# Attention and two feed-forward layers: the first layer's weights held in SBUF and its products fused, instead of streamed blocks of seven products

## The chip, the cores and the metric

The kernel runs on one core of one Trainium2 chip. The metric is the device time of one execution in microseconds (us). The kernel before took 1274.12 us, the median of three runs (1273.81 to 1278.1).

## The reference

All inputs are float64 or float32 arrays; the result is a 2304 x 512 array in float32.

```python
def _attn_ref(q, k, v, tau):                 # q, k, v: (4, 8, 576, 64)
    scores = scale * np.matmul(q, k.transpose(0, 1, 3, 2))
    thresh = np.max(scores, axis=-1, keepdims=True) - tau
    scores = np.where(scores >= thresh, scores, -1000000000.0)
...
    return np.matmul(attn, v).astype(np.float32)

def _moe_ref(x, w_in, w_out, alpha):         # (2304,512) (512,2048) (2048,512)
    h = x @ w_in
    g = np.maximum(h, 0.0) + alpha * np.minimum(h, 0.0)
    return (g @ w_out).astype(np.float32)

def _moe2_ref(x, w_in, w_out):
    h = x @ w_in
    g = np.where(h > 0.0, h, alpha * (np.exp(np.minimum(h, 0.0)) - 1.0))   # alpha = 1
    return (g @ w_out).astype(np.float32)
```

The heads of the attention are joined to a 2304 x 512 array, which goes through the first layer (`_moe_ref`) and then the second (`_moe2_ref`).

## The kernel before

**Attention** (lines 292 to 512). A unit is one pair of heads of one batch, and has nine jobs; each job makes scores on TensorE (PE), exponentials on ScalarE (ACT), a mask on VectorE (DVE), a scaling on GpSimd (POOL), then turns the result on PE and multiplies it with the values. `attention` writes all stages into a list with a place each and emits them sorted by place. At 144 places it calls `beside`, which converts weights for the layers. The result goes to DRAM as `x_d`.

**Weights.** They are 64-bit floats in DRAM. `single` (line 140) turns a piece of 128 x 512 into a 32-bit `x`: two ACT passes, three DVE passes, one POOL addition, on a piece that `load_piece` has brought two pieces ahead. `conversion` (line 168) splits `x` into a high and a low part (both fp32r) so that a product in full precision becomes three matmuls: high by high, high by low, low by high. For weights that are used in seven products it takes two pieces, forms the sums `s1` to `s4` and stores seven split blocks to DRAM (`in_d`, `out_d`, called `wi` and `wo` in the profile) with `store` (line 208, the DMA at line 211); for the plain product it stores the split piece to `whole_d` (`wp`). All split blocks go through two `split` buffers. `convert_step` runs the conversion from one `yield` to the next; the first twelve groups (`EARLY`) are converted beside the attention, the rest beside the first layer, one step per unit of the order below.

**Layers.** The 2304 tokens are three superchunks of 768, each handled as two halves of 384. The first product of a layer (`first_product`, line 562) takes blocks of 2 x 2 and needs seven products of blocks instead of eight, of six matmuls each; a partial sum in a PSUM bank is copied away by ACT (`keep`: `c1`, `u`, `w`) before the next product is added into the same bank. The second product of the first layer is plain (`plain_product`, line 676): per `f` (one of 16 blocks of 128 hidden columns) and half, `Split` makes high and low of the hidden block (`th`, `tl`) and twelve matmuls follow. The second layer has seven products in both (`second_product`, line 710). Split weights come from DRAM for every superchunk, in units of up to 1 MB, into a ring of four buffers (`wring`): `release(k)` (line 286) is called where the last matmul of unit `k` is issued and queues the load of unit `k + 4`, which on SyncE's queue (SP) waits until PE is done with the buffer. The first layer's result goes to DRAM (`y_d`) and is read back as operands (`load_operands`, line 529) of the second.

**Order.** `sequence` (line 768) lists the block products and gives each a length of 1 or 2 units, six matmuls being 1. Every helper step is put at a place relative to those (`put`), and `layers` (line 792) emits all sorted by place. On PE, DVE, ACT and POOL this order is fixed (`Pinned`, line 83; so the profile has line 89 for all of them); only DMA issues on SP may be moved by the scheduler. A step at the head of an engine's queue that waits holds up all behind it.

Of the kernel before, what the change touches and what calls it, by code (L numbers as in the profile page):

```python
# [20 lines left out]
def sparse_attention_two_mlps(  # L21
# [13 lines left out]
    nc = tc.nc  # L35
# [18 lines left out]
    EARLY = 12  # L54
    BESIDE = 144
# [4 lines left out]
    wring = ctx.enter_context(tc.tile_pool(name="wring", bufs=4))  # L60
    inp = ctx.enter_context(tc.tile_pool(name="inp", bufs=1))
# [13 lines left out]
    y_d = [dram.tile([P, KDM, SC], F32, name=f"y{n}") for n in range(NSC)]  # L75
    in_d = [[dram.tile([P, 7, 2, HM], F32, name=f"wi{y}_{p}") for p in range(FP)] for y in range(2)]
    out_d = [dram.tile([P, FP, 2, HM], F32, name=f"wo{i}") for i in range(7)]
    whole_d = [dram.tile([P, 2, 2, DM], F32, name=f"wp{j}") for j in range(FP)]
# [32 lines left out]

# [5 lines left out]
    groups = ([(0, 0, p) for p in range(FP)] + [(0, 1, f) for f in range(KFF)]  # L117
              + [(1, part, p) for part in range(2) for p in range(FP)])
    pieces = [(layer, part, f) for layer, part, p in groups
              for f in ((p,) if (layer, part) == (0, 1) else (p, p + FP))]  # L120
# [19 lines left out]
    def single():  # L140
# [8 lines left out]
        yield None  # L149
# [17 lines left out]

    def conversion(g):
        layer, part, p = group = groups[g]
        busy = g < EARLY  # L170
        if (layer, part) == (0, 1):
            for x in single():
                yield
            split = stage.tile([P, 2, DM], F32R, tag="split", name="split", bufs=2)
            high_of(act, split[:, 0], x)
            yield
            difference(dve, split[:, 1], x, split[:, 0].bitcast(F32))
            yield
# [18 lines left out]
        def high(n):  # L197
            products, of = made[n]
            split[n] = stage.tile([P, 2, 2, HM], F32R, tag="split", name="split", bufs=2)
            high_of(dve if busy and n < 2 else act, split[n][:, 0:len(products), 0, :], of[:, 0:len(products)])  # L200

        def low(n):
            products, of = made[n]
            many = len(products)
            difference(pool if busy and n % 2 else dve, split[n][:, 0:many, 1, :], of[:, 0:many],
                       split[n][:, 0:many, 0, :].bitcast(F32))

        def store(n):
            for i, product in enumerate(made[n][0]):
                to = in_d[layer][p][:, IN_ORDER.index(product)] if part == 0 else out_d[product - 1][:, p]  # L210
# [41 lines left out]
    def parts_of(n, part):  # L252
        return [(n, part, i, h) for i in range(FP if part == 0 or n < NSC else 7) for h in range(2)]

    units_of = []
    for n in range(2 * NSC):
        units_of += parts_of(n, 0)
        if n < NSC:
# [6 lines left out]
    def load_weights(k):  # L265
# [9 lines left out]
        elif layer == 0:  # L275
            for f in (2 * h, 2 * h + 1):
                convert_until((0, 1, f))
# [606 lines left out]
```

## Time and profile before

| what | us |
|---|---|
| runs: median (lowest to highest) | 1274.12 (1273.81 to 1278.1) |
| profiled execution, its own time | 1281.65 |
| profiled execution, its span | 1279.9 |
| PE busy | 1116.5 (87%) |
| DVE, ACT, POOL busy | 854.6 (67%), 732.9 (57%), 294.3 (23%) |
| DMA moved | 312.26 MB, 244 GB/s over the span |

The profile is of one execution, whose own time and span are 1.75 us apart. It has three stages: attention from 0 to 377 us, the first layer from there to 923.45 us (the first matmul on operands of the second layer), the second layer to 1275.5 us. A busy time of PE holds overlapping matmuls; how fast they run is better read from their starts. All engines' work stands under line 89, so instructions are told apart by their tiles: `psh` is a PSUM bank of a layer, `xh`, `xl` the split operands of a first product, `th`, `tl` those of a second, `g` a hidden block, `w` a ring buffer, `y` the first layer's result in DRAM.

### The profile page before, as it was taken

What the parts mean: (1) busy time and instruction counts of PE and PEld (TensorE: products, weight loads), DVE (VectorE), ACT (ScalarE), POOL (GpSimd) and SP (SyncE); (2) the same over time, 40 slices, a digit from 0 to 9 for tenths busy, and PEclk for the clock granted to TensorE, in tenths of its full rate; (3) what the DMA queues carried; (4) which work ended last, traced back from release to release, by engine and by line L of the source; (5) the groups of instructions that cost most, each with busy time, mean ns of one, the idle gap of its engine ahead of it and who ended that gap; (6) DMA issues with size and microseconds to landing.
All of it is one profiled execution on the core that took longest, in us unless ns stands there. A gap on an engine that the chain in (4) does not pass through costs nothing.

```text
span 1279.9 us, 20421 instructions
## 1 busy us (share of the span) xinstructions
PE 1116.5 (87%) x6872; PEld 958.6 (75%) x6872; DVE 854.6 (67%) x1781; ACT 732.9 (57%) x1531; POOL 294.3 (23%) x454
## 2 busy tenths in 40 slices
PE   4999999998979876868867776878999999999998
PEld 2555555555549866868857776878999999999998
DVE  2888788888756775536656545664267857885765
ACT  2888778777755553335435324533267657665663
POOL 1666666766642221101101100100000000000000
PEclk9999999999999988878888888988999999999999
DMA  6477555544339999778888889887877886787775
GB/s 140 116 209 217 159 160 150 171 129 136 122 117 314 357 322 320 265 263 302 297 299 290 284 292 305 300 282 265 286 254 276 289 287 253 283 287 254 253 277 178
DMA packets 173735, 312.26 MB, mean 244 GB/s; under 512 B 88896, under 2 KB 120128, under 8 KB 155968
## 3 DMA queue, kind: packets, MB, share of 16 engines
q1 hardware_dynamic: 173632, 310.96, 72.4%
q8 instruction: 55, 0.90, 0.3%
q14 instruction: 48, 0.39, 0.1%
HBM read 244.33 MB, written 66.58 MB: 243 GB/s over the span
## 4 chain that ended last, share of the span: by engine, by line
PE 54%; DMA 13%; DVE 13%; ACT 9%; POOL 5%; issue 4%; SPq 2%; POOLq 0%; DVEq 0%; ACTq 0%
PE psh L89 42%; PE pst L89 9%; DMA wi<-split 5%; DMA wo<-split 5%; PE ps L89 3%; POOL x L89 3%; DVE g L89 2%; DVE x L89 2%; DVE split L89 2%; ACT e L89 2%; ACT split L89 2%; DVE e L89 2%; ACT pt L89 2%; DVE st L89 2%; DMA y<-o 2%
## 5 line engine op out<-in xcount | busy, mean ns | idle before, releaser
L89 PE MATMUL psh<-xh,w 128*128 128x384 f32 x1344 | 361.4, 347 | 51.5 <-ACT u L89 30.5
L89 PEld LDWEIGHTS psh<-xh,w 128*128 128x128 f32 x1344 | 254.1, 196 | 57.5 <-ACT u L89 32.5
L89 PE MATMUL psh<-th,w 128*128 128x384 f32 x768 | 220.7, 368 | 46.0 <-ACT th L89 46.0
L89 PE MATMUL psh<-xl,w 128*128 128x384 f32 x672 | 231.4, 344 | 0.0
L89 PEld LDWEIGHTS psh<-th,w 128*128 128x128 f32 x768 | 157.7, 212 | 49.0 <-ACT th L89 48.9
L89 POOL TENSOR_TENSOR x<-x,t 128x512 uint32<-128x512 uint32 x64 | 88.9, 1389 | 422.1 <-DVE x L89 326.0
L89 PE MATMUL psh<-w,th 128*128 128x256 f32 x1008 | 178.2, 279 | 0.0
L89 PE MATMUL psh<-tl,w 128*128 128x384 f32 x384 | 143.1, 373 | 17.4 <-DVE tl L89 16.7
L89 PEld LDWEIGHTS psh<-w,th 128*128 128x128 f32 x1008 | 154.2, 188 | 0.0
L89 DVE SCALAR_TENSOR_TENSOR tl<-g,th 128x384 fp32r<-128x384 f32 x216 | 121.7, 572 | 36.1 <-ACT th L89 35.5
L89 PE MATMUL psh<-w,tl 128*128 128x256 f32 x504 | 141.2, 280 | 0.0
L89 ACT ACTIVATE t<-g 128x384 f32<-128x384 f32 x144 | 75.4, 523 | 105.6 <-DVE g L89 105.3
L89 ACT ACTIVATE th<-g 128x384 fp32r<-128x384 f32 x216 | 109.5, 518 | 45.0 <-PE psh L89 41.6
L89 PEld LDWEIGHTS psh<-xl,w 128*128 128x128 f32 x672 | 131.9, 196 | 0.0
L89 PEld LDWEIGHTS pst<-ident,e 128*128 128x128 f32 (+1 forms) x720 | 74.7, 138 | 75.8 <-issue 30.4
L89 DVE TENSOR_REDUCE st<-ps 128x1 f32<-128x576 f32 x144 | 107.9, 750 | 34.3 <-PE ps L89 33.8
L89 DVE SCALAR_TENSOR_TENSOR e<-ps,st,e 128x576 f32<-128x576 f32 x144 | 116.6, 809 | 17.7 <-ACT e L89 9.1
L89 PE MATMUL pst<-ident,e 128*128 128x128 f32 (+1 forms) x720 | 115.4, 286 | 12.4 <-ACT xt L89 3.6
L89 PE MATMUL ps<-kt,qt 64*128 64x288 f32 (+1 forms) x640 | 113.0, 462 | 9.2 <-DVE e L89 8.8
L89 POOL TENSOR_SCALAR e<-e,st 128x576 f32<-128x576 f32 x144 | 115.5, 806 | 23.4 <-DVE st L89 16.8
L89 ACT ACTIVATE e<-ps,st 128x576 f32<-128x576 f32 x144 | 106.9, 743 | 24.2 <-DVE st L89 23.6
L89 ACT ACTIVATE pt<-pst 128x512 f32<-128x512 f32 (+2 forms) x240 | 108.7, 463 | 17.7 <-PE pst L89 16.2
(69 smaller groups left out, 1543.4 us busy)
## 6 DMA issues: line engine op xcount, KB each, us to landing
w<-wi SPq DMA_DIRECT2D x48, 1024.0 KB, 7.2
w<-wp SPq DMA_DIRECT2D x48, 1024.0 KB, 6.7
w<-wo SPq DMA_DIRECT2D x42, 1024.0 KB, 5.8
w<-wi SPq DMA_DIRECT2D x48, 768.0 KB, 5.4
wi<-split SPq DMA_DIRECT2D x112, 256.0 KB, 2.6
r<-in_moe_w_in_dram SPq DMA_DIRECT2D x32, 512.0 KB, 4.7
r<-in_moe_w_out_dram SPq DMA_DIRECT2D x32, 512.0 KB, 5.5
wo<-split SPq DMA_DIRECT2D x56, 256.0 KB, 5.2
```

What stands on the lines that cost most here:

```text
L89: return lambda *args, **named: tc.keep_in_program_order(made(*args, **named))
```

## The change

The first layer is no longer done in seven products. Its 32 weight pieces are split straight into 16 SBUF blocks (`wt[f]`, 8 KB a partition, of the pools `wq`, `wx`, `wb`) and stay there; nothing of it is stored to DRAM or streamed. The tokens are six chunks of 384. Per chunk and `f`, `hidden_block` does twelve matmuls into a bank of its own, ACT and DVE make the activation and its split (`t`, `g`, `gh`, `gl`), and `outer_block`, two blocks later (`LAG`), does twelve matmuls into four banks (`psa`) that gather over all 16 `f`. The chunk's input is split once (`ih`, `il`; `load_in`), its result leaves through two `o` buffers. Twenty pieces (`FIRST` = 10 blocks) are converted beside the attention, the other twelve in the first 54 units of the layer, the sixteen groups of the second layer in the rest of it.

The second layer keeps its products and its ring. The ring buffers are the weight blocks 0 to 3 (`wq`), taken over as the last chunk is through with them; its split operands lie in blocks 4 to 9 (`wx`, `xs_of`), its hidden blocks in 10 to 15 (`wb`, `gs_of`) and one more tile. Its working tiles are in a pool (`mlp2`) that is opened when the first layer's pools are closed, and the first superchunk's operands are made during the last 20 units of the first layer.

```diff
-    wring = ctx.enter_context(tc.tile_pool(name="wring", bufs=4))
-    inp = ctx.enter_context(tc.tile_pool(name="inp", bufs=1))
+    wps = [ctx.enter_context(tc.tile_pool(name="wq", bufs=RING)), ctx.enter_context(tc.tile_pool(name="wx", bufs=FIRST - RING))]
+    inp = ctx.enter_context(tc.tile_pool(name="inp", bufs=3))
+    first_layer = ctx.enter_context(ExitStack())
+    inps = [first_layer.enter_context(tc.tile_pool(name="in0", bufs=1))]
...
-    groups = ([(0, 0, p) for p in range(FP)] + [(0, 1, f) for f in range(KFF)]
+    groups = ([(0, part, f) for f in range(KFF) for part in range(2)]
               + [(1, part, p) for part in range(2) for p in range(FP)])
...
-            difference(dve, split[:, 1], x, split[:, 0].bitcast(F32))
-            yield
-            nc.sync.dma_start(out=whole_d[p // 2][:, p % 2], in_=split.bitcast(F32))
+            if part == 0:
+                wt[p] = new_block(p)
+            hi, lo = wt[p][:, part, 0, :], wt[p][:, part, 1, :]
+            high_of(dve if p < FIRST else act, hi, x)
+            if p >= FIRST:
+                yield
+            difference(dve, lo, x, hi.bitcast(F32))
             stored.add(group)
...
+    def add_tile(blocks, pool_of):
+        blocks.tiles.append(pool_of.tile([P, 4 * DM], F32R, tag="w", name="w"))
+
+    def operand(product, kb):
+
+        i = 2 * (2 * (product - 1) + kb)
+        return xs_of[i], xs_of[i + 1]
...
+    def hidden_block(c, f, put, ends):
+        held = {}
+        start, done = ends["h", c, f]
+
+        def multiply():
+            held["h"] = ps = ps_first[0].tile([P, 512], F32, tag="h", name="psh")[:, 0:HT]
+            i = 0
+            for kk in range(KDM):
+                for wpart, xpart in ((0, 0), (0, 1), (1, 0)):
+                    pe.matmul(out=ps, lhsT=wt[f][:, 0, wpart, kk * P:(kk + 1) * P], rhs=ins[c][xpart][:, kk],
+                              start=(i == 0), stop=(i == 3 * KDM - 1))
+                    i += 1
...
+        def high():
+            gs[c, f] = [mlp.tile([P, HT], F32R, tag=tag, name=tag, bufs=LAG + 1) for tag in ("gh", "gl")]
+            act.activation(out=gs[c, f][0], in_=held["g"], func=AF.Copy)
+
+        def low():
+            difference(dve, gs[c, f][1], held["g"], gs[c, f][0].bitcast(F32))
+
+        put(start, multiply)
+        for dt, step in ((0.15, negative), (0.8, join), (1.5, high), (2.1, low)):
+            put(done + dt, step)
...
+    def outer_block(c, f, put, ends):
+        start, done = ends["o", c, f]
+
+        def multiply():
+            if f == 0:
+                accs[c] = [ps_first[1].tile([P, 512], F32, tag="a", name="psa")[:, 0:HT] for _ in range(KDM)]
+            hi, lo = gs.pop((c, f))
+            for m in range(KDM):
+                for i, (wpart, g) in enumerate(((0, hi), (1, hi), (0, lo))):
+                    pe.matmul(out=accs[c][m], lhsT=wt[f][:, 1, wpart, m * P:(m + 1) * P], rhs=g,
+                              start=(f == 0 and i == 0), stop=(f == KFF - 1 and i == 2))
+
+        def result(m):
+            o = mlp.tile([P, HT], F32, tag="o", name="o", bufs=2)
+            if m % 2 == 0:
+                act.activation(out=o, in_=accs[c][m], func=AF.Copy)
+            else:
+                dve.tensor_copy(out=o, in_=accs[c][m])
+            nc.sync.dma_start(out=y_d[c][:, m, :], in_=o)
+
+        put(start, multiply)
+        if f == KFF - 1:
+            for m in range(KDM):
+                put(done - 0.3 + (0.4 if c + 1 < NCH else 0.05) * m, result, m)
+        if c == NCH - 1:
+            if f < RING:
+                put(done + 0.3, load_weights, f)
+            elif f < FIRST:
+                put(done + 0.3, add_tile, xs_of, wps[1])
...
+        for c in range(NCH):
+            for f in range(KFF + LAG):
+                order += [("h", c, f)] if f < KFF else []
+                order += [("o", c, f - LAG)] if f >= LAG else []
+        for n in range(NSC):
+            for p in range(FP):
+                order += [(n, 0, p, 1), (n, 0, p, 2), (n, 0, p - 1, 3), (n, 0, p, 6), (n, 0, p - 1, 4),
+                          (n, 0, p, 7), (n, 0, p, 5)]
+            rounds = [(n, 1, product, p) for product in OUT_ORDER for p in range(FP)]
+            order += rounds[0:2] + [(n, 0, FP - 1, 3)] + rounds[2:4] + [(n, 0, FP - 1, 4)] + rounds[4:]
...
+                    put(ends["ho"[part], 0, f][0] - 0.05, convert_until, (0, part, f))
+        if c + 1 < NCH:
+            steps = load_in(c + 1)
+            for i in range(KDM + 3):
+                put(ends["h", c, 6][0] + 4.05 * i, next, steps, None)
+    begin = ends[0, 0, 0, 1][0]
+    for i in range(4 * KFF):
+        put(0.85 * i + 0.45, convert_step, len(groups))
+    steps = 13 * KFF
+    for i in range(steps):
...
+        steps = operand_steps(n)
+        for i in range(38):
+            if n == 0:
+                put(ends["o", NCH - 1, FIRST - 1][1] + 0.5 + 0.5 * i, next, steps, None)
+            else:
+                put(ends[n - 1, 0, FP - 1, 4][1] + 0.6 + 1.25 * i, next, steps, None)
+    run(begin)
+    convert_until(groups[-1])
+    staging.close()
+    first_layer.close()
+    mlp = ctx.enter_context(tc.tile_pool(name="mlp2", bufs=1))
+    for _ in range(KFF - FIRST):
+        add_tile(gs_of, wps[2])
+    gs_of.tiles.append(mlp.tile([P, 2 * HT], F32R, tag="g", name="g"))
+    ps_h.append(ctx.enter_context(tc.tile_pool(name="ps_8", bufs=8, space=PSUM)))
+    run(float("inf"))
```

SP's queue in the middle of the first layer, before: `w<-wp` is a load of streamed weights into a ring buffer that PE must have left, `wo<-split` a store of converted weights of the second layer.

```order
L283 DMA w<-wp_117 128x2048
L211 DMA wo_112<-split 128x512
L211 DMA wo_113<-split 128x512
L211 DMA wo_114<-split 128x512
L211 DMA wo_110<-split 128x512
L283 DMA w<-wp_119 128x2048
L283 DMA w<-wp_118 128x2048
L283 DMA w<-wp_120 128x2048
L211 DMA wo_108<-split 128x512
L283 DMA w<-wp_121 128x2048
```

With the change the same part of the layer has only the loads of pieces (`r`) and the stores:

```order
L137 DMA r_7176<-in_moe_w_out_dram 128x512
L219 DMA wo_109<-split 128x512
L219 DMA wo_110<-split 128x512
L219 DMA wo_112<-split 128x512
L219 DMA wo_113<-split 128x512
L219 DMA wo_114<-split 128x512
L219 DMA wo_115<-split 128x512
L219 DMA wo_111<-split 128x512
L137 DMA r_7355<-in_moe_w_out_dram 128x512
L137 DMA r_7401<-in_moe_w_out_dram 128x512
```

The loads that waited for PE are gone from between the stores.

PE in the first product of the first layer before: six matmuls into one bank, then the next product.

```order
L89 MATMUL psh_6194<-xl_5749,w_6114 128x384
L89 MATMUL psh_6194<-xh_5748,w_6114 128x384
L89 MATMUL psh_6288<-xh_5373,w_6175 128x384
L89 MATMUL psh_6288<-xl_5374,w_6175 128x384
L89 MATMUL psh_6288<-xh_5373,w_6175 128x384
L89 MATMUL psh_6288<-xh_5663,w_6175 128x384
L89 MATMUL psh_6288<-xl_5664,w_6175 128x384
L89 MATMUL psh_6288<-xh_5663,w_6175 128x384
L89 MATMUL psh_6301<-xh_5533,w_6175 128x384
```

With the change, the end of one hidden block, the outer block of two `f` earlier, and the next hidden block:

```order
L93 MATMUL psh_5472<-il_4584,w_4373 128x384
L93 MATMUL psh_5472<-ih_4583,w_4373 128x384
L93 MATMUL psa_5141<-gh_5422,w_3625 128x384 x2
L93 MATMUL psa_5141<-gl_5423,w_3625 128x384
L93 MATMUL psa_5142<-gh_5422,w_3625 128x384 x2
L93 MATMUL psa_5142<-gl_5423,w_3625 128x384
L93 MATMUL psa_5143<-gh_5422,w_3625 128x384 x2
L93 MATMUL psa_5143<-gl_5423,w_3625 128x384
L93 MATMUL psa_5144<-gh_5422,w_3625 128x384 x2
L93 MATMUL psa_5144<-gl_5423,w_3625 128x384
L93 MATMUL psh_5515<-ih_4583,w_4476 128x384
```

No bank of a hidden block is written by a second product, so PE no longer follows an ACT copy at once; the two matmuls that share `gh` stand side by side.

The place where the first layer ends and the second begins, on ACT and then on SP (with the semaphores that each waits for; `DMAHW` ones are those of DMAs): `o_8558` and `o_8564` are the first and third copy of the last chunk's result, `c1_8603` the second layer's first copy out of PSUM.

```order
L93 ACTIVATE w_8226<-w_8226 128x384 [waits DMAHW7_49]
L93 ACTIVATE o_8558<-psa_7925 128x384 [waits PE_49]
L93 ACTIVATE o_8564<-psa_7927 128x384 [waits DMAHW2_49,PE_49,Activation_49]
L93 ACTIVATE c1_8603<-psh_8589 128x384 [waits DMAHW3_49,DMAHW1_49,DMAHW4_49,DMAHW0_49,DMAHW5_49,DVE_49,DMAHW6_49,PE_49,Activation_49]
L93 ACTIVATE t_8612<-w_8579 128x384 [waits DVE_49]
```

```order
L219 DMA wo2_111<-split_8364 128x512 [waits DMAHW1_49]
L623 DMA y5_100<-o_8558 128x384 [waits DMAHW2_49,Activation_49]
L623 DMA y5_100<-o_8561 128x384 [waits DMAHW3_49,DVE_49]
L623 DMA y5_100<-o_8564 128x384 [waits DMAHW4_49,Activation_49]
L623 DMA y5_100<-o_8567 128x384 [waits DMAHW5_49,DVE_49]
L276 DMA w_8621<-wi2_103 128x2048 [waits DMAHW6_49,PE_49]
```

`o_8564` waits for the DMA of `o_8558`, the second y DMA's `o_8561` is likewise what DVE's `o_8567` waits for, and `c1_8603` waits among others for the DMAs of `o_8561`, `o_8564` and `o_8567`, since its pool lies where the first layer's buffers were.

## Rows read from the trace of the kernel before

**Rows 1.** Busy time by stretch: us, PE, PEld, DVE, ACT, POOL (instructions); clock, DMA share, GB/s
```profile
0.00:377.00 377.00, 332.03 (x2193) 189.51 (x2193) 289.38 (x663) 278.21 (x569) 229.71 (x409) 1.00 0.53 151
377.00:923.45 546.45, 432.07 (x2160) 417.53 (x2161) 311.42 (x617) 235.29 (x485) 64.61 (x45) 0.88 0.84 296
382.00:450.00 68.00, 63.44 (x345) 60.88 (x346) 47.28 (x90) 39.76 (x84) 13.06 (x8) 0.98 0.93 336
923.45:1275.50 352.05, 352.05 (x2520) 351.43 (x2520) 252.81 (x499) 219.41 (x479) 0.00 (x0) 1.00 0.77 265
```

**Rows 2.** PE's waits in the first layer: us in total, times, longest us
```profile
PE psh L89 <- ACT th L89: 46.0, 9, 6.8
PE psh L89 <- ACT u L89: 30.5, 6, 7.2
PE psh L89 <- ACT w L89: 17.6, 8, 6.9
PE psh L89 <- DVE tl L89: 16.7, 9, 6.5
```

**Rows 3.** ACT's waits on stores of converted weights, whole span
```profile
ACT split L89 <- DMA wi<-split: 69.0, 15, 14.6
...
ACT split L89 <- DMA wo<-split: 65.0, 14, 12.3
```

**Rows 4.** Waits of SP's DMA queue in the first layer
```profile
SPq L283 <- PE psh L89: 149.3, 73, 5.2
```

**Rows 5.** PE's instructions in order of time: start us, us, what [idle before it]
```profile
382.16 0.69 PE L89 MATMUL psh<-xh,w 128*128 128x384 f32 x1 [2.84 <-ACT c L89]
...
870.11 0.69 PE L89 MATMUL psh<-th,w 128*128 128x384 f32 x1 [4.44 <-ACT th L89]
...
871.44 0.84 PE L89 MATMUL psh<-th,w 128*128 128x384 f32 x2
...
876.24 0.74 PE L89 MATMUL psh<-th,w 128*128 128x384 f32 x2
...
880.12 0.51 PE L89 MATMUL psh<-th,w 128*128 128x384 f32 x2
...
911.84 0.51 PE L89 MATMUL psh<-th,w 128*128 128x384 f32 x2
```

**Rows 6.** Groups of instructions, whole span: busy us, mean ns | idle before
```profile
L89 DVE SCALAR_TENSOR_TENSOR tl<-g,th 128x384 fp32r<-128x384 f32 x216 | 121.7, 572 | 36.1 <-ACT th L89 35.5
...
L89 ACT ACTIVATE th<-g 128x384 fp32r<-128x384 f32 x216 | 109.5, 518 | 45.0 <-PE psh L89 41.6 <-DVE tl L89 2.5 <-DVE g L89 0.5
...
L89 DVE TENSOR_SCALAR x<-x 128x512 f32<-128x512 f32 (+1 forms) x128 | 57.7, 451 | 8.4 <-ACT x L89 6.2
...
L89 DVE SCALAR_TENSOR_TENSOR x<-r,x 128x512 uint32<-128x512 uint32 x64 | 44.5, 696 | 0.6
...
L89 DVE SCALAR_TENSOR_TENSOR split<-x,split 128x512 fp32r<-128x512 f32 (+1 forms) x56 | 34.1, 610 | 26.8 <-ACT split L89 26.8
...
L89 ACT ACTIVATE t<-psh 128x384 f32<-128x384 f32 x48 | 22.8, 476 | 0.0
...
L89 DVE SCALAR_TENSOR_TENSOR s<-x 128x256 f32<-128x256 f32 x48 | 22.7, 473 | 21.1 <-POOL x L89 21.0
...
L89 DVE SCALAR_TENSOR_TENSOR g<-t,alpha,psh 128x384 f32<-128x384 f32 x24 | 14.5, 606 | 0.0
```

**Rows 7.** Stores to wi during the attention, 25 to 345 us: their landing
```profile
DMA to landing us min/median/max: 2.0/2.4/6.6
```

**Rows 8.** DMAs to and from y, whole span: their landing
```profile
DMA to landing us min/median/max: 1.9/5.4/8.3
```

**Rows 9.** Attention between its start-up and its last jobs, 25 to 345 us, as Rows 1
```profile
25.00:345.00 320.00, 295.34 (x1975) 168.66 (x1975) 267.64 (x614) 251.93 (x514) 212.07 (x372) 0.99 0.55 157
```

More of the change, by code (lines that the diff above doesn't have):

```diff
@@ L116, in sparse_attention_two_mlps @@
     BOTTOM = float.fromhex("0x1.0p-15")
-    groups = ([(0, 0, p) for p in range(FP)] + [(0, 1, f) for f in range(KFF)]
+    groups = ([(0, part, f) for f in range(KFF) for part in range(2)]
               + [(1, part, p) for part in range(2) for p in range(FP)])
-    pieces = [(layer, part, f) for layer, part, p in groups
-              for f in ((p,) if (layer, part) == (0, 1) else (p, p + FP))]
+    pieces = [(layer, part, f) for layer, part, p in groups for f in ((p,) if layer == 0 else (p, p + FP))]
+    wt = {}
     staged, stored = {}, set()
@@ L199, in high @@
             split[n] = stage.tile([P, 2, 2, HM], F32R, tag="split", name="split", bufs=2)
-            high_of(dve if busy and n < 2 else act, split[n][:, 0:len(products), 0, :], of[:, 0:len(products)])
+            high_of(act, split[n][:, 0:len(products), 0, :], of[:, 0:len(products)])
         def low(n):
@@ L204, in low @@
             many = len(products)
-            difference(pool if busy and n % 2 else dve, split[n][:, 0:many, 1, :], of[:, 0:many],
+            difference(dve, split[n][:, 0:many, 1, :], of[:, 0:many],
                        split[n][:, 0:many, 0, :].bitcast(F32))
@@ L209, in store @@
             for i, product in enumerate(made[n][0]):
-                to = in_d[layer][p][:, IN_ORDER.index(product)] if part == 0 else out_d[product - 1][:, p]
+                to = in_d[p][:, IN_ORDER.index(product)] if part == 0 else out_d[product - 1][:, p]
                 nc.sync.dma_start(out=to, in_=split[n].bitcast(F32)[:, i])
@@ L574, in multiply @@
             for kb in range(2):
-                x = operands[n, product, kb]
+                x = operand(product, kb)
                 for wpart, xpart in ((0, 0), (0, 1), (1, 0)):
@@ L594, in bend @@
         def bend(fh, th, src=None):
-            f = p + fh * FP
             held = {}
@@ L753, in second_product @@
                 start, end = ends[n, 1, product, p]
-                g = Split(lambda product=product, p=p: operand(product, p))
+                g = Split(lambda product=product, p=p: block(product, p))
                 g.put(put, start)
@@ L790, in sequence, with put, run @@
         return ends
-    def layers():
-        todo, ends = [], sequence()
-        def put(at, what, *args):
-            todo.append((at, len(todo), what, args))
-        def stop_staging():
-            convert_until(groups[-1])
-            staging.close()
-            late.append(ctx.enter_context(tc.tile_pool(name="late", bufs=1)))
-        for n in range(2 * NSC):
-            for p in range(FP):
-                first_product(n, p, put, ends)
-            (plain_product if n < NSC else second_product)(n, put, ends)
-            if n + 1 < 2 * NSC:
-                steps = operand_steps(n + 1)
-                base = ends[n, 0, FP - 1, 4][1]
-                for i in range(46):
-                    put(base + 1.0 + 1.05 * i, next, steps, None)
-        begin = ends[NSC, 0, 0, 1][0]
-        for i in range(int(begin)):
-            put(i + 0.45, convert_step, len(groups))
-        put(begin + 4.0, stop_staging)
-        for _, _, what, args in sorted(todo, key=lambda t: t[:2]):
+    todo = []
+    def put(at, what, *args):
+        todo.append((at, len(todo), what, args))
+    def run(before):
+        todo.sort(key=lambda t: t[:2])
+        while todo and todo[0][0] < before:
+            _, _, what, args = todo.pop(0)
             what(*args)
```

232 lines of the change are left out of this document (98 added, 134 removed).

## The prediction

> **What bounds the kernel now.** I read the busy time by stage first. The second layer is PE's own: PE is busy for 352.05 of 352.05 us at full clock [rows 1], so a change there can only add. In the attention PE is busy for 295.34 of 320 us [rows 9]; little is to be had. The first layer is the loose one: 546.45 us for 2160 matmuls at a mean granted clock of 0.88, with DMA at 0.84 of its engines' time [rows 1]. What it would take with PE fed is read from its last stretch: from 880.12 to 911.84 us a pattern of three matmuls repeats 61 times without a gap, so 183 matmuls take 31.72 us, 173.3 ns each at 384 columns [rows 5]. 2160 of them are 374.4 us, so 172 us of the layer are not PE's work. Of these 111 us are the four largest waits of PE, 94 of them for ScalarE, up to 7 us at a time [rows 2]. The rest is mostly the clock after such a wait: behind an idle 4.44 us, 15 matmuls from 871.44 to 876.24 us take 320 ns each [rows 5], the pace of the lower of its two levels (1.2 against 2.4 GHz), 2.2 us lost there.
>
> Why ScalarE is late stands in its own waits: 134 us, 29 times, 4.6 us on average, for a store of converted weights that must leave a `split` buffer [rows 3]. And why the stores are late in SP's queue: 149.3 us of it are spent on weight loads that wait for PE to leave a ring buffer [rows 4]; the stores stand behind them. It is a circle: PE waits for ScalarE, ScalarE for a store, the store for a load, the load for PE.
>
> **The change part by part.** All against the profiled execution (span 1279.9, own time 1281.65 us), which is 0.6% above the median of the runs, 1274.12.
>
> *Attention.* PE's work is the same. Beside it, twenty pieces are converted as before, but without the sums `s1` to `s4` and without stores to DRAM; the operand steps of seven products give way to one input chunk. PE idles 24.7 of 320 us there [rows 9], which is the most that it can gain. A loss is possible too, since the converted pieces' last steps now follow each other on VectorE; I bound it at 2 us, a tenth of that idle time. I take 3 us gained, near the small end, since the softmax chain, in which PE waits, stays.
>
> *First layer, PE.* 6 chunks x 16 `f` x 24 matmuls are 2304, 144 more than before. At 173.3 ns that is 399.4 us. Here a rule can be weighed: the Trainium skill, TensorE: Matmul & The Clock Gate, section "Wait — 56ns, not 53.3ns?", gives a start-to-start time of the columns at 2.4 GHz plus about 2.5 ns, 162.5 ns for 384, and by it the term would be 374 us; the trace does not agree (173.3 ns with no gap and full clock), and the trace is taken.
>
> *First layer, the circle.* Loads that wait for PE are gone from SP's queue, and DMA has pieces, stores, inputs and results only. So a store should land as in the attention, in 2.4 us [rows 7]. A block's chain from its bank to the split is 0.48 + 0.61 + 0.52 + 0.57 = 2.2 us [rows 6], and four blocks of twelve matmuls (8.3 us) lie between a hidden block's end and the outer block that needs it: 6.1 us of slack, more than the 4.6 us of a mean stall today. VectorE's load for the whole layer: 96 blocks x 1.18 us (112 us), twelve pieces x (2 x 0.451 + 0.696 + 0.610 = 2.21 us, 27 us), sixteen groups x (twice 1.60 us for unpacking, four sums of 0.473, four splits of 0.610: 7.5 us, 120 us), about 25 us for inputs, results and the second layer's operands, 284 us of some 409: 70%, as in the second layer now (252.81 of 352.05 [rows 1]), where PE never waits. So I take PE as the bound and add three losses:
>
> - The first chunk. Five steps of 0.85 units (a unit is six matmuls, 1.04 us) make a piece every 4.4 us; VectorE is then 2.21 of 4.4 plus 1.18 of 4.16 us busy, 78%. The nearest row is 382 to 450 us, where nine pieces are converted with VectorE at 70%: 345 matmuls, worth 59.8 us, take 68, 8.2 us lost [rows 1]. For twelve pieces that is 11 us; with the slack of 6.1 us, against today's copies which PE awaits a unit later, it can be 0. I take 5.
> - Five chunk ends. The third and fourth copy of a result wait for the DMA of the first and second, with ScalarE and VectorE held. Three hidden blocks (6.2 us) run meanwhile. With 2.4 us to landing the next split is there in time; with the 5.4 us that y's DMAs take now [rows 8] it comes 2.4 us late, and the clock costs a little more: 0 to 15 us for five, I take 3, since DMA will be lighter.
> - Stalls of later chunks that pass the slack: 0 to 15 us, I take 2, for the same reason.
>
> First layer 409.4 us, 137 less than 546.45. That includes the entry, where PE now idles 2.84 us at 382.16 for a copy `c1` [rows 5]; no copy is awaited there with the change.
>
> *From the first layer to the second.* The new wait. `c1`, the second layer's first copy, waits for the last y DMAs. The second copy of the last result ends about when PE does; its DMA lands 2.4 us later plus some 0.3 for the issue, the fourth copy takes 0.5, its DMA again 2.7, `c1` 0.5: 6 us after PE's last matmul of the layer. PE has products 1 and 2 to do (12 matmuls, 2.1 us), then product 6 adds into the bank that `c1` copies. So 4 us idle, and about 2 for the clock, as behind the 4.44 us above: 6 us. With landings of 1.9 us it is 3, with 5.4 us 13 [rows 8]. Queued behind `c1` on ScalarE are only the next copies of the same layer. VectorE's operand steps (22 of 0.57 us in 20 units, with the last blocks) fit, but barely.
>
> *Second layer.* The same 2520 matmuls, ring and copies; operands are read in place, and the loads stand where PE has left the blocks. 352 us stays; VectorE and ScalarE as now hide all else. If that cover fails, a wait of a few us per superchunk shows.
>
> Sum: -3 (attention) - 137 (first layer) + 6 (start of the second) = -134 us: a span of 1146 and, from the median of the runs, **1140 us**.
>
> **The rivals.**
>
> *The conversions set the pace.* If ScalarE, VectorE and GpSimd, which wait for each other in a piece, run the whole layer at the pace of 382 to 450 us, 68 for 59.8 [rows 1], it takes 454 us: 45 us more, 1185. For it: the density in the first chunk is higher than there. Against it: afterwards a step comes every 1.6 us, and the slack is longer than any copy's now.
>
> *The circle is not broken* (slower). If the stores are late for their own sake and not for the loads before them, the 172 us remain, the 144 extra matmuls add 25 us and the second layer's start 6: with 3 us gained in the attention 28 us slower, 1302. It decides where a store takes more than about 6 us to land with ScalarE behind it on every group. Against it: the stores of the attention land in 2.4 us [rows 7] with the same two buffers.
>
> *Matmuls closer together.* The new blocks take two matmuls in a row on one moving operand; if that saved the 11 to 13 ns above the array time of 160 ns, 25 us more would be gained, 1115. No row shows a closer spacing at full clock. The page named above has it.
>
> That the change does not do what it says is excluded: no load of first-layer weights is in SP's order.
>
> **How the numbers follow.** The forecast has 0.79, its own range being 1122 (no loss but 3 us at the start of the second layer, 8 us gained in the attention) to 1170 (all upper ends but that of the later chunks). The pace of the conversions has 0.14, and its milder forms fill 1170 to 1185; the unbroken circle 0.03, the closer matmuls 0.02, and 0.02 stays for what I do not see, half of it near no change. The range of 1122 to 1182 leaves out the upper half of the first rival, the other two and the unseen: 2 in 10 at most. About 0.5% is what a measurement of this kernel can tell from no change. Faster 0.96, same 0.01, slower 0.03.
>
> **What would show it.** The first layer: PE's starts 173 ns apart in long runs, granted clock near 1.00, no wait of SP for PE but at the chunk's end, stores landing in 2 to 3 us, DMA's share about halved. The step at the start of the second layer: one wait of PE for `c1` of about 4 us. Wrong would be: many waits of PE for `gl` or `gh`, a clock under 0.95 in the first layer, or waits of PE in the second layer beyond its first products.

## The result, and the profile after

The changed kernel takes **1145.11 us** (median of 4 runs, 1144.36 to 1147.49), the kernel before beside it 1276.11 us (1273.81 to 1278.29): a ratio of 0.8977, 95% interval 0.8952 to 0.9002. The forecast was 1140 us, in a range of 1122 to 1182. The profiled execution after spans 1142.6 us; the sum of the prediction had 1146. So the number held. One link of the mechanism behind it did not, as the runs below show. A time given without a number of runs is that of one execution; the kernel before, measured beside them, took 1269.31 to 1282.86 us.

Busy time by stretch after the change; the columns are those of [rows 1], the stretches are the attention, the first layer, a window of 41.6 us around the end of its first chunk, and the second layer:

```profile
0.00:364.17 364.17, 328.96 (x2193) 188.98 (x2193) 275.76 (x621) 265.53 (x540) 208.95 (x394) 0.98 0.39 99
364.17:780.23 416.06, 407.17 (x2306) 401.49 (x2305) 264.53 (x518) 200.17 (x403) 59.16 (x44) 1.00 0.46 158
405.60:447.20 41.60, 35.45 (x175) 31.46 (x176) 25.74 (x48) 19.27 (x39) 9.00 (x7) 0.96 0.44 142
780.23:1138.20 357.97, 357.19 (x2518) 356.08 (x2519) 252.94 (x498) 221.25 (x478) 0.00 (x0) 1.00 0.75 259
```

Against [rows 1]: the first layer 416.06 instead of 546.45 us with 144 matmuls more, its granted clock 1.00 instead of 0.88, DMA's share 0.46 instead of 0.84. The attention ends 12.8 us earlier. The second layer is 6 us longer with the same matmuls.

PE's waits from 364 us to the end (us in total, times, longest), where 111 us stood in [rows 2]:

```profile
PE psa L93 <- ACT gh L93: 4.9, 6, 1.6
PE psh L93 <- ACT o L93: 2.2, 1, 2.2
PE psa L93 <- DVE gl L93: 1.8, 4, 1.0
PE psh L93 <- DVE tl L93: 0.6, 2, 0.3
PE psh L93 <- ACT c L93: 0.2, 1, 0.2
```

ScalarE's waits in the first layer, those that bear on PE; the waits for stores of converted weights are 20 us, where [rows 3] had 134 us over the whole span:

```profile
ACT w L93 <- POOL x L93: 24.4, 11, 3.2
ACT o L93 <- DMA y<-o: 14.3, 6, 3.6
ACT split L93 <- DMA wi<-split: 10.4, 6, 4.2
...
ACT split L93 <- DMA wo<-split: 9.3, 6, 3.4
```

DMA issues in the first layer, 364 to 780 us (count, KB each, median us from issue to landing):

```profile
wi<-split SPq DMA_DIRECT2D x56, 256.0 KB, 2.3
wo<-split SPq DMA_DIRECT2D x56, 256.0 KB, 2.3
...
y<-o SPq DMA_DIRECT2D x23, 192.0 KB, 1.9
```

The same stores in the first layer of the kernel before, 382 to 930 us:

```profile
wi<-split SPq DMA_DIRECT2D x56, 256.0 KB, 4.4
wo<-split SPq DMA_DIRECT2D x56, 256.0 KB, 5.2
```

A store lands in 2.3 us, forecast 2.4. But beside the loads before, it took 4.4 to 5.2 us *after its issue*, and that time is not spent in SP's queue. SP's waits ahead of the stores (line 211) in the first layer before, 377 to 923 us, say the same:

```profile
SPq L211 <- DVE split L89: 85.0, 32, 6.8
```

SP stood ready at a store and waited for VectorE to finish the split. When each of the 112 stores of this layer is paired in order with the end of its split, the trace has 0.7 us from there to the issue on average (over 2 us for 9 of them) and 5.3 us from the issue to the landing. The stores were late, but hardly behind a load in the queue. This is where the runs start.

### The profile page after: what moved, and what is told of

Its sections match the earlier page's. It is cut to its first block, busy times and chain, and to the rows that moved or that the text cites. A ratio compares the mean times of both kernels' runs of the same rounds, so it can differ in the third digit from the quotient of the medians.

```text
span 1142.6 us, 20027 instructions
## 1 busy us (share of the span) xinstructions
PE 1093.8 (96%) x7016; PEld 946.8 (83%) x7016; DVE 794.3 (70%) x1639; ACT 686.9 (60%) x1421; POOL 268.1 (23%) x438
## 4 chain that ended last, share of the span: by engine, by line
PE 79%; ACT 7%; DVE 6%; issue 3%; POOL 2%; SPq 2%; DMA 1%; DVEq 0%; POOLq 0%; ACTq 0%
PE psh L93 46%; PE psa L93 15%; PE pst L93 14%; PE ps L93 5%; ACT e L93 2%; ACT pt L93 2%; POOL x L93 2%; DVE x L93 1%; DVE st L93 1%; DVE e L93 1%; DVE w L93 1%; ACT t L93 1%; ACT w L93 1%; ACT x L93 0%; SPq L304 0%
## 5 line engine op out<-in xcount | busy, mean ns | idle before, releaser
L93 PE MATMUL psh<-ih,w 128*128 128x384 f32 x768 | 210.3, 337 | 0.0
L93 PE MATMUL psa<-gh,w 128*128 128x384 f32 x768 | 197.1, 338 | 4.9 <-ACT gh L93 4.9
L93 PE MATMUL psh<-w 128*128 128x384 f32 x1008 | 176.8, 334 | 2.4 <-ACT o L93 2.2
L93 PEld LDWEIGHTS psh<-w 128*128 128x128 f32 x1008 | 174.3, 188 | 3.3 <-ACT o L93 2.5
L93 PEld LDWEIGHTS psa<-gh,w 128*128 128x128 f32 x768 | 138.9, 188 | 7.1 <-ACT gh L93 6.8
L93 PEld LDWEIGHTS psh<-ih,w 128*128 128x128 f32 x768 | 140.5, 188 | 0.1
L93 PE MATMUL psa<-gl,w 128*128 128x384 f32 x384 | 130.6, 340 | 1.8 <-DVE gl L93 1.8
L93 PE MATMUL psh<-il,w 128*128 128x384 f32 x384 | 129.1, 336 | 0.0
L93 DVE SCALAR_TENSOR_TENSOR e<-ps,st,e 128x576 f32<-128x576 f32 x144 | 116.7, 811 | 13.1 <-POOL st L93 7.5
L93 ACT ACTIVATE t<-psh 128x384 f32<-128x384 f32 x120 | 58.0, 484 | 86.9 <-PE psh L93 86.2
L93 DVE SCALAR_TENSOR_TENSOR g<-t,alpha,psh 128x384 f32<-128x384 f32 x96 | 58.8, 612 | 57.5 <-ACT t L93 57.2
```

The costliest lines, as they stand in the source:

```text
L93: return lambda *args, **named: tc.keep_in_program_order(made(*args, **named))
```

## The experiments

All first layers are measured on PE's timeline, from its first matmul of the layer to the first of the next.

**1. Is it the place in SP's queue?** The kernel before, its stores moved to another queue:

```diff
-                nc.sync.dma_start(out=to, in_=split[n].bitcast(F32)[:, i])
+                nc.scalar.dma_start(out=to, in_=split[n].bitcast(F32)[:, i])
-            nc.sync.dma_start(out=whole_d[p // 2][:, p % 2], in_=split.bitcast(F32))
+            nc.scalar.dma_start(out=whole_d[p // 2][:, p % 2], in_=split.bitcast(F32))
```

> The kernel before, with the stores of converted weights issued from ScalarE's own DMA queue instead of SP's; order of the work on PE, VectorE and GpSimd as it was. Theory (circle: the stores stand in SP's queue behind weight loads that wait for PE): a store now waits for nothing but its split, so ScalarE's 134 us of waits for stores fall below 40 us, the first layer from 546 to 430 to 480 us, the whole to 1170 to 1220. Rival 1 (DMA's engines are the bound, 0.84 busy in the first layer): the same bytes move, the layer stays above 520 us, the whole within 25 us of 1274. Rival 2 (too little slack between a copy and the matmuls that need it): stalls stay, the layer above 500 us.

Measured: 1291.18 us (before beside it 1279.15). The first layer takes 539.4 us (392.55 to 931.93) instead of 546.5, and the attention 16 us more, with ScalarE's DMA issues in its order. The stores land later than before, and ScalarE still waits 112 us for them in 382 to 930 us:

```profile
wi<-split ACTq DMA_DIRECT2D x56, 256.0 KB, 5.5
wo<-split ACTq DMA_DIRECT2D x56, 256.0 KB, 5.7
```

```profile
ACT split L89 <- DMA wo<-split: 61.7, 16, 8.4
ACT split L89 <- DMA wi<-split: 50.4, 13, 7.9
```

So the theory fell: no store stood behind a waiting load any more, and the layer stayed. The run is not a clean one, though: a DMA that ScalarE issues also waits in ScalarE's order for VectorE's part of the split, and about 20 us of such short waits are new there. The Trainium skill, DMA: Bandwidth & Descriptors, section "Issuing engines are not separate DMA queues", says that DMAs issued from different engines share the same 16 DMA engines and interleave there. The run agrees as far as it goes: in the other queue landings of 4.4 and 5.2 us became 5.5 and 5.7, not shorter.

**2 to 4. Slack and stream.** One step less between a hidden block and its outer block; then the changed kernel made to read its blocks again from DRAM (run 3, "the streamed run" from here on); then both.

```diff
-    LAG = 2
+    LAG = 1
-        for dt, step in ((0.15, negative), (0.8, join), (1.5, high), (2.1, low)):
+        for dt, step in ((0.15, negative), (0.8, join), (1.5, high), (1.95, low)):
```

> The changed kernel with an outer block one step instead of two behind its hidden block, so the slack between a split and the matmuls that read it falls from 6.1 to about 2 us (its VectorE step is put 0.15 units earlier to stand ahead of them). Theory (circle): with no load in SP's queue that waits for PE a store lands in 2.3 us, so less slack costs the first chunk and a wait of some 2 us at each chunk's start: first layer 416 to 440 us, the whole 1146 to 1170. Rival (the gain came from the deeper slack): copies are late in all chunks as before, first layer 470 us or more, the whole above 1195.

Measured: 1160.19 us, first layer 432.2 us. The layer loses 16 us, as expected; the deeper slack alone is not the gain.

```diff
...
+            nc.sync.dma_start(out=back_d[p][:, part], in_=wt[p][:, part].bitcast(F32))
             stored.add(group)
...
+        if c < NCH - 1:
+            put(done + 0.3, lambda: nc.sync.dma_start(out=wt[f].bitcast(F32), in_=back_d[f]))
         if c == NCH - 1:
```

> The changed kernel, but the first layer's converted weights are also stored to DRAM and read back into the same blocks after each outer block, in five of six chunks: 84 MB of loads that wait for PE in SP's queue and 17 MB of stores come back, about what the change saved of DMA's work (312 to 195 MB). Slack stays at two steps. Theory (circle): the loads hold back stores and inputs again; part of the loss returns, first layer 430 to 480 us; what the slack of 6 us covers stays away. Rival 1 (slack alone made the gain): 416 to 422 us as in the changed kernel. Rival 2 (the lighter load of DMA made the gain): first layer above 500 us. If the stores made the attention slower in the kernel before, its end is at 370 us or later instead of 364.

> Both edits together: weights read back into the blocks, and an outer block one step behind. Theory (circle, which costs where the slack is shorter than a store that waits behind a load): now nothing hides the stalls, first layer 480 to 550 us, much more than the sum of the two single losses. Rival (each counts for itself): the two single losses add up, within 10 us.

Measured: streamed 1215.7 us, first layer 486.8 us (363.94 to 850.73); with the short slack 1253.45 us, first layer 525.2 us. So bringing the traffic back brings 71 us of the 130 back, though the slack of two steps stays: more than the circle's range of 430 to 480 us, less than the second rival's 500. With one step it is 109 us, 22 more than the two single losses (71 and 16) together. The attention ended at 363.94 us although ten blocks' stores lay in it: stores are not what it gained. The streamed run's DMA in 364 to 850 us:

```profile
w<-wb SPq DMA_DIRECT2D x80, 1024.0 KB, 8.5
wi<-split SPq DMA_DIRECT2D x56, 256.0 KB, 4.3
wo<-split SPq DMA_DIRECT2D x56, 256.0 KB, 5.0
```

The landings of before are back. The loads bring a wait for PE and megabytes; the next runs separate them.

**5. The waits without the bytes.** Against the streamed run, in part; what is stored to be read back shrinks likewise:

```diff
-            put(done + 0.3, lambda: nc.sync.dma_start(out=wt[f].bitcast(F32), in_=back_d[f]))
+            put(done + 0.3, lambda: nc.sync.dma_start(out=wt[f][:, 1, 1, DM - 64:DM].bitcast(F32), in_=back_d[f]))
```

> The changed kernel with 80 loads after the outer blocks as in the streamed run, at the same places in SP's queue and with the same wait for PE, but of 32 KB each (the last 64 columns of a block's second half, stored once) instead of 1024 KB. So SP waits for PE as there, and DMA moves next to nothing more. Theory A (the circle as predicted: the stores are late because they stand in SP's queue behind loads that wait for PE): the first layer as in the streamed run, 470 to 490 us, the whole above 1195. Theory B (the stores are late in DMA's engines, behind the megabytes of those loads; formed after the run with ScalarE's own queue, where the first layer stayed at about 540 us): 416 to 425 us, the whole 1143 to 1153.

Measured: 1144.82 us, first layer 416.2 us. SP waited longer for PE than in the streamed run (48 us there), and it cost nothing; the stores landed as in the changed kernel:

```profile
SPq L633 <- PE psa L94: 82.9, 47, 3.9
```

```profile
wi<-split SPq DMA_DIRECT2D x56, 256.0 KB, 2.3
wo<-split SPq DMA_DIRECT2D x56, 256.0 KB, 2.4
```

**6. The bytes without the waits, first try.** Against the streamed run, in part:

```diff
-            put(done + 0.3, lambda: nc.sync.dma_start(out=wt[f].bitcast(F32), in_=back_d[f]))
+            put(done + 0.3, lambda: nc.sync.dma_start(out=idle_d[f], in_=back_d[f if c else f % FIRST]))
```

> The other half: 80 copies of 1024 KB each at the same places in SP's queue, from DRAM to a DRAM buffer that nothing reads, so none of them waits for PE; the first layer's weights are stored as in the streamed run, and its matmuls read the blocks kept in SBUF. Theory A (queue order): 416 to 425 us, the whole 1143 to 1153. Theory B (DMA's engines): stores land in 4 to 6 us instead of 2.3, ScalarE waits for them, and the first layer takes 460 to 490 us, the whole 1185 to 1215.

Measured: 1148.6 us, first layer 421.1 us: a loss of 5, in the range of theory A. But the copies did not keep their places. They wait for nothing but the stored weights, and DMA issues on SP are not held in program order, so the scheduler moved many of them ahead: the first was issued at 76.9 us and the last at 682.7, 35 of the 80 beside the attention and 45 in the first layer.

```profile
L633 SPq DMA_DIRECT2D wz<-wb x80: 467/513/1543, 76.9 to 682.7; - x80
```

Where they did run, from 450 to 690 us, DMA was as busy and moved as much as in the streamed run (the columns of [rows 1]; this run first), and PE hardly lost time:

```profile
450.00:690.00 240.00, 235.32 (x1348) 234.06 (x1347) 146.90 (x293) 111.22 (x226) 30.74 (x23) 1.00 0.92 327
```

```profile
450.00:690.00 240.00, 207.18 (x1097) 201.06 (x1096) 120.19 (x239) 89.97 (x187) 24.25 (x18) 0.93 0.90 328
```

The stores landed sooner than beside loads into SBUF, in 3.9 us on average in that window against 5.4. Their medians over the first layer:

```profile
wi<-split SPq DMA_DIRECT2D x56, 256.0 KB, 3.5
wo<-split SPq DMA_DIRECT2D x56, 256.0 KB, 3.1
```

So DMA engines that are 0.92 busy are not by themselves the cause, and the question of the loads into SBUF stays open; run 11 asks it again.

**7. Twice the room for stores, in the kernel before.**

```diff
-            split[n] = stage.tile([P, 2, 2, HM], F32R, tag="split", name="split", bufs=2)
+            split[n] = stage.tile([P, 2, 2, HM], F32R, tag="split", name="split", bufs=4)
-            split = stage.tile([P, 2, DM], F32R, tag="split", name="split", bufs=2)
+            split = stage.tile([P, 2, DM], F32R, tag="split", name="split", bufs=4)
```

> The kernel before with four split buffers instead of two, so that ScalarE meets a store twice as late as now. Both theories: ScalarE's 134 us of waits for stores fall to under 40 us. If those waits are what makes PE late, the first layer falls from 546 to 440 to 490 us and the whole to 1165 to 1220. Rival (DMA's 0.84 of its engines' time is the bound of the layer, and the next wait, for a piece's load, takes their place): the layer stays above 515 us, the whole above 1240.

Measured: 1207.89 us (before beside it 1274.78), first layer 477.3 us (372.35 to 849.68), 69 less. All that is left of ScalarE's waits for stores, and the longest waits of PE, in 360 to 850 us:

```profile
ACT split L89 <- DMA wo<-split: 0.2, 1, 0.2
```

```profile
PE psh L89 <- DVE tl L89: 21.9, 10, 6.5
PE psh L89 <- ACT u L89: 19.1, 2, 9.5
PE psh L89 <- ACT th L89: 14.1, 4, 4.9
PE psh L89 <- DMA w<-wi: 7.5, 5, 2.2
```

And DMA in 382 to 805 us, at 352 GB/s:

```profile
q1 hardware_dynamic: 47818, 148.51, 95.5%
```

Here ScalarE's waits for stores are shown to be a cause: without them 69 us of the 172 are gone, and 4.6 us in the attention, although the stores now land in 7.7 and 7.8 us. The rest is not taken apart: PE still waits for VectorE and ScalarE, for loads too (9.5 us), and with the stall relaxed DMA runs at 0.955 of its engines' time. That makes the traffic a likely second bound just below the first; no run tries it in this kernel.

**9 and 11. Without the stand in the queue, then without the wait.** The streamed kernel with the stores of weights and results on ScalarE's queue; and, apart from that, the streamed kernel with its loads 10 units after the outer block, when PE has left it.

```diff
-                nc.sync.dma_start(out=to, in_=split[n].bitcast(F32)[:, i])
+                nc.scalar.dma_start(out=to, in_=split[n].bitcast(F32)[:, i])
-            nc.sync.dma_start(out=y_d[c][:, m, :], in_=o)
+            nc.scalar.dma_start(out=y_d[c][:, m, :], in_=o)
```

> The streamed run again (weights read back into the blocks, slack of two steps, first layer 487 us there), with the stores of converted weights and of results issued from ScalarE's own DMA queue, so that none of them stands behind a load that waits for PE; the megabytes stay. Theory A (both are needed: the stand in SP's queue and a long landing add up to more than the slack): without the stand the first layer falls to 416 to 445 us, the whole to 1143 to 1175. Theory B (landing alone: the stores wait in DMA's engines behind 1024 KB loads): 470 to 490 us, above 1195. In between would mean that each has a part. The attention may lose up to 3 us, as ScalarE waits there for VectorE before a store.

Measured: 1244.08 us, first layer 515.6 us, worse than in the one queue (486.8) and outside both ranges. The stores' landings, 364 to 880 us:

```profile
wi<-split ACTq DMA_DIRECT2D x56, 256.0 KB, 6.5
wo<-split ACTq DMA_DIRECT2D x56, 256.0 KB, 6.4
```

Part of the 29 us more is of the edit's own making. ScalarE now waits in its order for what its DMA issues need from VectorE, waits that the streamed run does not have:

```profile
ACT t L94 <- DVE o L94: 16.2, 3, 5.7
...
ACT t L94 <- DVE s L94: 13.2, 8, 2.2
```

The run with the late loads has this edit against the streamed one:

```diff
-            put(done + 0.3, lambda: nc.sync.dma_start(out=wt[f].bitcast(F32), in_=back_d[f]))
+            put(done + 10.0, lambda: nc.sync.dma_start(out=wt[f].bitcast(F32), in_=back_d[f]))
```

> The streamed run (first layer 487 us) with each load of 1024 KB put 10 units (about 10 us) after its outer block instead of 0.3, so that PE has left the block when SP comes to the load; 40 us remain before PE reads it again. Same bytes into SBUF, same queue, hardly a wait of SP for PE (48 us of such waits in the streamed run; here below 10). Theory B (the stores' landing, 4.3 to 5.0 us beside loads of 1024 KB instead of 2.3, passes what the two split buffers hide; waits in the queue don't matter): 470 to 500 us, the whole above 1195, landings of 4 us or more. Theory A (loads that wait for PE are needed for the loss; for it speaks the run that copied from DRAM to DRAM without such waits and lost 4 us): 416 to 440 us, the whole below 1170.

Measured: 1215.24 us, first layer 485.8 us, the streamed run's loss to 1 us, with 6.9 us left of SP's waits for PE at these loads; then DMA's issues:

```profile
SPq L632 <- PE psh L94: 4.2, 7, 1.3
SPq L632 <- PE psa L94: 2.7, 8, 0.6
```

```profile
w<-wb SPq DMA_DIRECT2D x80, 1024.0 KB, 8.3
wi<-split SPq DMA_DIRECT2D x56, 256.0 KB, 5.2
wo<-split SPq DMA_DIRECT2D x56, 256.0 KB, 4.7
```

That settles it for the streamed kernel: waits without bytes cost nothing (5), and loads into SBUF without waits are enough for the whole loss (11). Paired as above, a store there is issued 0.6 us after its split in the streamed run and 0.4 in run 11, against 0.3 in the changed kernel. Runs 1 and 9 fit, with the reservations made there. The loss goes with the stores' landing, 2.6 us on average in the changed kernel's first layer, 3.8 for 5 us lost (6), and 5.3 to 5.4 for 70 (3, 11). What it is in loads into SBUF that holds a store up for longer than copies from DRAM to DRAM at the same DMA share is not shown. Not separated is how much of the 70 is waits for result stores (42 us of ScalarE's in the streamed run) and how much for converted weights (94 us).

**8, 10 and 12. What is left.** Two edits in the second layer; then these and one in the first chunk; then that with another pace.

```diff
-            o = mlp.tile([P, HT], F32, tag="o", name="o", bufs=2)
+            tag = "t" if c == NCH - 1 and m > 1 else "o"
+            o = mlp.tile([P, HT], F32, tag=tag, name=tag, bufs=2)
...
     mlp = ctx.enter_context(tc.tile_pool(name="mlp2", bufs=1))
+    shift = mlp.tile([P, 8], F32, name="shift")
+    nc.vector.memset(shift, 0.0)
```

> The changed kernel with two edits of the second layer that show at different places. (a) The last chunk's third and fourth result copies go to the two t buffers, free by then, instead of waiting for the DMAs of the first two: PE's wait of 2.2 us before product 1 falls to 0 to 0.7 us. (b) An unused tile of 32 bytes at the head of the second layer's buffers, which puts th and tl at 32 instead of 0 modulo 64 bytes, as in the kernel before. If the address sets the pace of the second products, 120.0 ns from matmul to matmul falls to 116.7 ns and the second layer from 358 to 353 us; if not, 120.0 ns stays. The whole: 1136 to 1139 with both, 1141 to 1143 with (a) alone.

Measured: 1139.79 us, just above the range. PE's wait before product 1 fell from 2.2 to 0.7 us, and the second products went from 120.0 to 118.3 ns a matmul, not to 116.7: the place of the buffers matters, but not in the way that the expectation had it.

```diff
-    shift = mlp.tile([P, 8], F32, name="shift")
+    shift = mlp.tile([P, 56], F32, name="shift")
...
+            if p >= FIRST:
+                yield
             if part == 0:
                 wt[p] = new_block(p)
...
-    for i in range(4 * KFF):
+    for i in range(72):
...
-        put(0.85 * 4 * KFF + (begin - 0.85 * 4 * KFF - 8) * i / steps + 0.45, convert_step, len(groups))
+        put(0.85 * 72 + (begin - 0.85 * 72 - 8) * i / steps + 0.45, convert_step, len(groups))
```

> The changed kernel with three edits. (a) The first chunk: a step more between GpSimd's addition and ScalarE's copy of it to a block (six steps a piece, 72 at 0.85 units), so that ScalarE no longer waits there with the copies for PE behind it; of the 13 us that the first layer takes above 2304 x 173.3 ns, 8 to 12 go, and its ScalarE waits for GpSimd's x (24 us in the layer) fall below 8. (b) The result copies of the last chunk in free buffers, as before: 1.5 us. (c) The second layer's buffers moved by 224 bytes, which puts th and tl at 480 modulo 512 bytes, as in the kernel before (at 256 they took 120.0 ns a matmul, at 288 118.0): 116.7 ns and 5 us if that address sets the pace, 118 to 120 ns if the kernel before had it from something else. The whole: 1127 to 1134 us, ratio to before 0.884 to 0.890.

Measured: **1133.3 us** (4 runs, 1132.2 to 1133.99), ratio to before 0.8899, interval 0.8873 to 0.8925, below the changed kernel's 0.8977 (0.8952 to 0.9002). The first layer takes 408.7 us, 7.3 less, of which the result copies are 1.5; the first chunk gave some 5.8, not 8 to 12. The new step brought the last pieces too near, and PE waits once for a copy of a weight block; ScalarE still waits 18 us for GpSimd, where under 8 were expected (PE's waits first, 364 to 780 us):

```profile
PE psh L93 <- ACT w L93: 2.5, 1, 2.5
```

```profile
ACT w L93 <- POOL x L93: 18.3, 9, 3.2
```

PE in the second products, after (first) and in this version, two rows 150 and 155 matmuls apart:

```profile
848.84 0.40 PE L93 MATMUL psh<-w,th 128*128 128x256 f32 x2
...
866.84 0.40 PE L93 MATMUL psh<-w,th 128*128 128x256 f32 x2
```

```profile
861.73 0.28 PE L93 MATMUL psh<-w,th 128*128 128x256 f32 x1
...
879.81 0.39 PE L93 MATMUL psh<-w,th 128*128 128x256 f32 x2
```

That is 120.0 and 116.6 ns. The second layer, from PE's first matmul to the end of the span, went from 362.4 to 359.3 us: 3 of the 5 us that were expected.

The last run is this version with each 0.85 replaced by 0.80, so that the first chunk's pieces come earlier:

> The version with three mends (1133.3 us) with the steps of the first chunk at 0.80 instead of 0.85 units, so that the last pieces are there 3 units earlier: there PE waited once, 2.5 us, for a copy to block 15, and the clock cost about 2 us behind it. Expected 1128 to 1131 us; if the tighter steps bring back ScalarE's waits for GpSimd, 1133 or more.

Measured: 1136.46 us (4 runs, 1136.17 to 1137.29), ratio 0.8903, interval 0.8883 to 0.8923. PE's wait for the copy is 1.6 instead of 2.5 us, but ScalarE waits 20.8 us for GpSimd, and the first layer is 411.8 us: the second branch of the expectation. The ratios of these two versions cannot be told apart.

## Why the prediction was right, and where it was wrong

The span fell by 137.3 us, forecast 134. By terms:

| term | forecast | measured | from |
|---|---|---|---|
| attention | -3 | -12.8 | first layer starts at 364.17, before 376.97 |
| first layer, to PE's last matmul | -137 | -132.6 | 416.06 less the 2.21 us at its end, against 546.45 |
| start of the second layer | +6 | +2.4 | PE's waits for `o` 2.2 and `c1` 0.2 |
| second layer | 0 | +5.7 | the rest; 1512 matmuls x 3.3 ns = 5.0 |

**PE as the bound of the first layer** held: 2304 matmuls, granted clock 1.00, and from 450 to 760 us hardly a gap. 399.4 us was the right base (from 499.80 to 519.79 us 115 matmuls start, 173.8 ns apart), and the rival of closer matmuls did not come.

**"The first layer, the circle" failed as a cause.** The prediction read SP's 149.3 us of waits for PE [rows 4] and put the stores' lateness on them ("the store for a load, the load for PE"). The trace of before has 0.7 us from a split's end to its store's issue, and runs 5 and 11 take the link apart. The stores were late because they took 5.3 us to land beside megabytes of loads into SBUF, with two buffers between ScalarE and them (run 7). The change takes away the loads, and with them both the wait and the traffic. Both mechanisms forecast the same time for it, so the size of the term came out right from a wrong link, and the measured time could not tell them apart. DMA's share of 0.84 stood in [rows 1] and was not weighed as a bound. The rival "the circle is not broken" named the true condition, stores late for their own sake, but took it to need more than about 6 us, where medians of 4.4 to 5.2 us were enough; it did not come, since the loads were gone.

**The first chunk** was the mis-sized term of the layer: 5 us forecast of 0 to 11. From 405.60 to 447.20 us PE does 175 matmuls where 240 of 173.3 ns fit, so 11 us are lost, at the upper bound. The 5 us were argued from VectorE's load; what showed is ScalarE's 24 us of waits for GpSimd's addition, all before 450 us, with the copies that PE awaits behind it. Only the rival on the conversions' pace spoke of these engines waiting for each other. Run 10 supports it (5.8 us less with 6 us less of these waits), without taking the rest away.

**Chunk ends and later stalls**, 3 and 2 us forecast, cost nothing that the profile shows.

**The conversions' pace**, the likeliest rival, did not set that of the whole layer: VectorE is busy for 264.53 us of 416, forecast 284 of 409.

**The start of the second layer** went by another chain than forecast. PE waited before product 1, for a bank, and `c1` was in time:

```profile
776.49 0.49 ACT L93 ACTIVATE o<-psa 128x384 f32<-128x384 f32 x1 [1.27 <-PE psa L93]
779.00 0.49 ACT L93 ACTIVATE o<-psa 128x384 f32<-128x384 f32 x1 [2.01 <-DMA y<-o]
782.19 0.49 ACT L93 ACTIVATE c<-psh 128x384 f32<-128x384 f32 x1 [2.70 <-DMA y<-o]
```

The third result copy waits 2.01 us for the DMA of the first; PE's next bank waits for it. Landings of 1.9 us made it 2.2 us, and PE ran on at full clock; the end of the forecast's range that had 1.9 us was 3.

**The attention** gained four times the 3 us. About 4.6 us belong to the waits for two split buffers (run 7); stores as such cost nothing there (runs 3, 9, 11). The other 8 may come from the sums and the other conversions that are gone; no run shows it.

**The second layer** was costed at nothing, as its matmuls are the same. Its second products ran at another pace, which no row of before could have told.

## What to carry to other kernels

A queue that waits in the profile is not yet the cause of what stands behind it. Look first at how long after its data is ready a DMA is issued, and compare its time from issue to landing in a quiet and in a busy stretch. Where the landing itself has doubled, as here, moving the issue to another queue did not help; fewer bytes and more buffers did. To separate a wait from its traffic, make the transfer tiny, or late, with the rest in place, and then see from the trace where the transfers really ran: in run 6 nearly half of them had moved elsewhere.

## What the hardware showed that was not expected

The pace of the same 256-column matmuls depends on where the second layer's buffers lie in SBUF. The medians of segments of 36 matmuls are 120.0 ns in the changed kernel and the seven runs with its layout, 118.3 ns where these buffers stand 32 bytes further (run 8), and 116.7 to 117.8 ns where they stand 224 bytes further (runs 10 and 12) and in the kernel before with its two variants. Of the operands of these matmuls only `th` and `tl`, the stationary ones, moved; `w`, the moving one, lies in the ring, which stayed. Whether their addresses set the pace or those of the other buffers moved with them stays open, and no trace lists addresses. The 384-column matmuls, at about 173 to 174 ns, read none of the moved buffers, so these runs say nothing of them. The 224 bytes made the second layer 3.1 us shorter, where 1512 x 3.4 ns would be 5.1; the difference is not explained.

The Trainium skill, SBUF — State Buffer, section "Operand start alignment", gives rules for which addresses are legal and says that speed was not timed there.
